# Sigmoid attention and a gated MLP on one core: group 0 loaded as FP32 by SyncE and cast on chip, and the first pass laid out anew

## The chip, the cores and the metric

The kernel runs on one core of a Trainium2 chip. The metric is the device time of one execution, in microseconds (us). The engines are TensorE (PE, matrix products into PSUM), VectorE (DVE), ScalarE (ACT), GpSimd (POOL) and SyncE (SP, which only issues DMAs here). Each engine has a queue of its own and works through it in order.

## The reference

```python
def _attn_ref(q, k, v):                    # q, k, v: 8 x 12 x 448 x 64, float32
    S = q.shape[2]
    scale = 1.0 / np.sqrt(q.shape[-1])
    scores = scale * np.matmul(q, k.transpose(0, 1, 3, 2)) - np.log(S)
    attn = 1.0 / (1.0 + np.exp(-scores))
    return np.matmul(attn, v).astype(np.float32)

def _moe_ref(x, w_in, w_out, beta):        # x: 3584 x 768, w_in: 768 x 2048, w_out: 2048 x 768
    h = x @ w_in
    g = h * (1.0 / (1.0 + np.exp(-beta * h)))
    return (g @ w_out).astype(np.float32)
```

The attention's output, with its heads side by side (3584 tokens of 768), is the MLP's x. There is no softmax: each score goes through a sigmoid by itself.

## The kernel before, in words

**Groups and visits.** The heads are taken four at a time: a group g is four heads of one batch, so there are 24 groups, three to a batch. A group's q and k are loaded with a cast from FP32 to FP16 by DMAs that POOL issues (`load_one`, L126), into a tile `raws[g]`. DVE transposes them (`transpose`: L207 for q, L216 and L220 for k). A visit is a set of score matmuls (L236) for one group and 128 of its keys, with the sigmoid on ACT behind it (`weigh`, L249, or `weigh_two`, L264) which reads the scores out of PSUM. The values (`attend`, L334) multiply the sigmoids by v, and DVE casts the results into `xTs` (L343), the input of the MLP. The last 64 keys of a head need v's last rows twice, in both halves of the partitions: `double_v_last` (L171) copies them.

**Dense matmuls.** All matmuls of the MLP stand in one list, `fill`, in a fixed order: x @ w_in (L356 for the first batches, L521 for the later ones), the gate (ACT L368 and L532, DVE L371 and L535, POOL L535), and the product with w_out (L386, L435, and L639 in a Strassen scheme). `fill_units(n)` issues the next n of them. They are put between the visits, so that PE works while ACT does the sigmoids.

**The first pass.** For batch 0, three groups, the order is written out by hand in the list `BEGIN`. A half visit (`half_visit`) covers half of a group's queries: `("scores", g, half, second)`, where second says which keys. `("q", g, half)` and `("k", g)` are transposes, `("values", g, half)` the values, `("dense", n)` n matmuls of `fill`, `("idle", n)` n zero matmuls. Zero matmuls (`idle_units`, L765) multiply a tile of zeros, 512 columns each, and their result is not used. Eleven stand ahead of everything, 12 more lie between the first half visits. The first dense matmuls need the values of all three groups for one half of the queries, so six half visits stand ahead of those; two more stand ahead of the dense ones in the list.

**Loads.** POOL issues group 0's first q half and its k before all else, then `LOADS` in order: groups 1 and 2, v, q's second halves, and the eight parts of w_in. `loads()` issues what follows (group 3, w_out, the next v). The DMAs of POOL share eight semaphores in turn, so the ninth waits for the first to have landed, and so on. SP issues the load of beta at the start, and the stores.

**Later visits.** From batch 1 on a loop over `visits` (numbered n) issues one visit, then as many dense matmuls as a pace asks for: what is left to do in the phase over the visits that are left. `MORE` adds to or takes from that number by visit, `LATE` says how many dense matmuls go ahead of the values in a visit, and `RESERVE` what is held back at the end of a phase. `first_layer` is a stretch in which x @ w_in of a pair of batches is done without visits.

**The end.** The last token tile is done by `single` (L435), whose second matmul group reads a sum of two halves of the gated values, made by DVE (L420) when the tile begins.

Of the kernel before, what the change touches and what calls it, by code (L numbers as in the profile page):

```python
# [13 lines left out]
def kernel(  # L14
# [10 lines left out]
    nc = tc.nc  # L25
# [175 lines left out]
    def transpose(g: int, r: int, c0: int = 0, c1: int = NB):  # L201
        raw = raws[g][:, r]
        if r == 0:
# [3 lines left out]
            nc.vector.transpose(  # L207
                out=in_order(g // QPB, qT[g][:, c0 * BLK : c1 * BLK]),
                in_=raw[:, c0:c1].rearrange("p c d -> p (c d)").bitcast(FP32),
            )  # L210
            return
# [393 lines left out]
    def hid(t: int, half: int):  # L605
        return gt[:, half * ND : (half + 1) * ND, cols(t)]
# [144 lines left out]
    with tc.manual_schedule():  # L751
        load_one(0, 0, 0, NH)
        load_one(0, 1)
        nc.gpsimd.memset(nlogs, NEG_LOG_S)
# [8 lines left out]
        def idle_units(n: int):  # L763
            for _ in range(n):
                nc.tensor.matmul(idle, still[:, 0:P], still, start=True, stop=True)  # L765

        idle_units(11)
        def load(what, *a):
            if what == "q":
                load_one(a[0], 0, a[1] * NH, (a[1] + 1) * NH)  # L770
            elif what == "k":
                load_one(a[0], 1)
            elif what == "v":
                load_v_full(0, a[0] * HQ, a[1] * HQ)
            elif what == "last":
                load_v_last(0)
            elif what == "w_in":
                load_w_in(*a)

        nc.sync.dma_start(out=beta_in[0:NDC], in_=moe_beta.rearrange("(c p) -> c p", p=P))  # L780
        LOADS = [
            ("q", 1, 0), ("k", 1), ("q", 2, 0), ("k", 2), ("last",), ("v", 0, 3), ("q", 0, 1), ("q", 1, 1),
            ("w_in", 0, 2), ("w_in", 2, 4), ("q", 2, 1), ("w_in", 4, 6), ("w_in", 6, 8), ("w_in", 8, 10),
            ("w_in", 10, 12), ("w_in", 12, 14), ("w_in", 14, 16),
        ]
        for x in LOADS:
            load(*x)

        def loads():
            load_qk(3)  # L790
            load_w_out(0, 0)
            load_w_out(1, 0)
            load_v(1)
            load_qk(4)
            load_qk(5)
            load_w_out(0, 1)
            load_w_out(1, 1)

        def beta_columns():
# [5 lines left out]
        BEGIN = [  # L805
            ("q", 0, 0), ("k", 0), ("q", 1, 0), ("scores", 0, 0, 1), ("idle", 4), ("k", 1), ("idle", 4),
            ("scores", 0, 0, 0), ("k", 2), ("q", 2, 0), ("scores", 1, 0, 0), ("idle", 4), ("v", 0),
            ("scores", 1, 0, 1), ("scores", 2, 0, 0), ("values", 0, 0), ("q", 0, 1), ("q", 1, 1),
            ("scores", 2, 0, 1), ("beta",), ("values", 1, 0), ("scores", 0, 1, 0), ("values", 2, 0),
            ("scores", 0, 1, 1), ("loads",), ("q", 2, 1), ("dense", 12), ("scores", 1, 1, 1), ("two",),  # L810
            ("dense", 6), ("scores", 1, 1, 0), ("dense", 18), ("scores", 2, 1, 0), ("values", 0, 1),
            ("values", 1, 1), ("scores", 2, 1, 1), ("dense", 9), ("values", 2, 1), ("dense", 42), ("k", 3),
            ("q", 3, 0), ("q", 3, 1), ("dense", 21),
        ]
        for what, *a in BEGIN:
# [5 lines left out]
            elif what == "scores":  # L821
                half_visit(a[0], a[1] * QH, a[2])
            elif what == "idle":
                idle_units(a[0])
# [34 lines left out]
        def left_us(n: int):  # L859
# [57 lines left out]
        for n, (g, jt, also) in enumerate(visits):  # L917
# [73 lines left out]
```

## Time and profile before

| | |
|---|---|
| median of 3 runs | 376.06 us (375.95 to 376.45) |
| profiled execution | 375.61 us |
| its span, first to last instruction | 373.8 us |
| PE busy | 365.7 us (98%) |
| ACT busy | 255.8 us (68%) |
| DVE busy | 254.2 us (68%) |
| POOL busy | 91.5 us (24%) |
| bytes read from HBM | 45.62 MB |

Times in the rows below are microseconds from the start of the span. A row of the timeline has the start, the time taken, the engine, the line, the operation, what it writes and reads, how many were merged (x16), and in brackets the idle time of the engine before it and what ended that. A row of the chain of waits has the start, the time taken and what the end of the kernel hung on then. The busy time of PE is modelled and has short waits in it. PEclk is the granted clock of TensorE, 1.00 at full speed.

### The profile page before, as it was taken

Reading aid. Unit: us, or ns where it says so; the run is one execution under the profiler, and the core shown is the slowest. Engines: PE = TensorE matmul, PEld = TensorE weight load, DVE = VectorE, ACT = ScalarE, POOL = GpSimd, SP = SyncE. Lnnn points to the kernel's source line nnn. Section 1 sums busy time; section 2 is a strip of 40 time slices with the busy share of each in tenths; the row PEclk is TensorE's granted clock in tenths of the full one; section 3 lists DMA queues with packets and bytes.
Section 4 is the critical chain, followed back from the end, with each engine's and each line's share of the span. In section 5 each row is a group of like instructions: output and inputs, shape, how many; then the busy total and the mean of one; then the engine's idle time right before and its main releaser. Section 6 shows DMA issues by size and latency. Waiting matters only on the chain.

```text
span 373.8 us, 7284 instructions
## 1 busy us (share of the span) xinstructions
PE 365.7 (98%) x2887; PEld 182.5 (49%) x2887; DVE 254.2 (68%) x478; ACT 255.8 (68%) x295; POOL 91.5 (24%) x138
## 2 busy tenths in 40 slices
PE   8899999999999999999999999999999999999996
PEld 3466544443444455544444445554444455555654
DVE  2444796776586967787666667778767667678661
ACT  3996865698967668886767748887678647882000
POOL 8743353141151013234123003235100002230000
PEclk9999999999999999999999999999999999999999
DMA  8999999993269030039839301028903111000333
GB/s 116 178 196 203 197 203 200 231 125 51 49 81 179 1 86 1 0 51 127 171 50 213 91 16 28 1 35 112 162 3 84 44 44 42 1 2 1 86 84 126
DMA packets 42545, 34.29 MB, mean 92 GB/s; under 512 B 21888, under 2 KB 39056, under 8 KB 42512
## 3 DMA queue, kind: packets, MB, share of 16 engines
q0 software_dynamic: 36976, 22.81, 44.6%
q1 hardware_dynamic: 5536, 11.02, 10.4%
q8 instruction: 22, 0.36, 0.4%
q14 instruction: 11, 0.09, 0.1%
HBM read 45.62 MB, written 11.01 MB: 151 GB/s over the span
## 4 chain that ended last, share of the span: by engine, by line
PE 91%; ACT 5%; DVE 2%; issue 1%; DMA 1%; POOL 0%; ACTq 0%; POOLq 0%
PE ps L639 26%; PE ps L521 26%; PE ps L236 11%; PE ps L334 9%; PE ps L356 9%; PE ps L386 4%; PE ps L435 4%; ACT attns L249 3%; ACT attns L264 1%; DMA raw<-in_k_dram 1%; ACT sg L368 1%; PE ps L765 0%; DVE sum L628 0%; DVE kT L216 0%; DVE qT L207 0%
## 5 line engine op out<-in xcount | busy, mean ns | idle before, releaser
L264 ACT ACTIVATE attns<-ps,nlogs 128x1792 f16<-128x1792 f32 x75 | 131.6, 1755 | 46.3 <-PE ps L236 46.0
L535 POOL TENSOR_TENSOR gt<-attns,sg 128x448 f16<-128x448 f32 x21 | 23.9, 1139 | 142.0 <-ACT sg L532 142.0
L639 PEld LDWEIGHTS <-sum 128*128 128x128 f16 x440 | 40.3, 98 | 36.9 <-issue 12.1
L236 PE MATMUL ps<-qT,kT 32*128 32x448 f16 (+3 forms) x864 | 51.9, 339 | 2.8 <-ACT attns L249 1.7
L532 ACT ACTIVATE sg<-ps,beta_sb 128x448 f32<-128x448 f32 x72 | 45.2, 632 | 8.6 <-PE ps L521 5.8
L521 PE MATMUL ps<-xT,w_in 128*128 128x448 f16 x216 | 49.2, 353 | 0.0
L521 PE MATMUL ps<-xT,w_S 128*128 128x448 f16 x216 | 49.2, 352 | 0.0
L639 PE MATMUL ps<-w_T,sum 128*128 128x384 f16 x264 | 48.5, 327 | 0.0
L535 DVE TENSOR_TENSOR gt<-ps,sg 128x448 f16<-128x448 f32 x72 | 44.3, 619 | 3.9 <-ACT sg L532 3.7
L343 DVE CAST xT<-ps 128x448 f16<-128x448 f32 (+1 forms) x54 | 28.9, 569 | 22.9 <-PE ps L334 22.7
L521 PEld LDWEIGHTS <-w_in 128*128 128x128 f16 x288 | 28.0, 98 | 26.6 <-issue 0.7
L657 DVE TENSOR_TENSOR osb<-ps,osb 128x384 f32<-128x384 f32 x55 | 30.5, 555 | 14.9 <-PE ps L639 12.9
L334 PE MATMUL ps<-attns,v 128*64 128x448 f16 (+3 forms) x432 | 40.5, 340 | 0.1
L356 PE MATMUL ps<-xT,w_in 128*128 128x448 f16 (+1 forms) x240 | 39.7, 316 | 0.6 <-DVE gt L371 0.6
L628 DVE TENSOR_TENSOR sum<-gt 128x1024 f16<-128x1024 f16 x55 | 36.5, 679 | 0.2
L126 POOL DMA_DIRECT2D raw<-in_q_dram x27 | 15.1, 558 | 80.2 <-DVE kT L220 72.6
L371 DVE TENSOR_TENSOR gt<-ps,sg 128x448 f16<-128x448 f32 (+1 forms) x40 | 20.0, 527 | 20.4 <-ACT sg L368 20.2
L639 PE MATMUL ps<-w_out,gt 128*128 128x384 f16 x176 | 33.3, 327 | 0.0
L639 PE MATMUL ps<-w_out,sum 128*128 128x384 f16 x176 | 32.2, 327 | 0.0
L581 DVE TENSOR_TENSOR ps<-ps,attns 128x448 f32<-128x448 f32 x24 | 15.2, 633 | 23.2 <-PE ps L521 22.4
L521 PEld LDWEIGHTS <-w_S 128*128 128x128 f16 x216 | 21.1, 98 | 19.4
L356 PEld LDWEIGHTS <-w_in 128*128 128x128 f16 x240 | 21.9, 98 | 17.1 <-issue 6.2
(51 smaller groups left out, 370.4 us busy)
## 6 DMA issues: line engine op xcount, KB each, us to landing
out_dram<-osb SPq DMA_DIRECT2D x100, 96.0 KB, 1.9
raw<-in_k_dram POOLq DMA_DIRECT2D x24, 224.0 KB, 5.6
raw<-in_q_dram POOLq DMA_DIRECT2D x21, 224.0 KB, 4.3
v<-in_v_dram POOLq DMA_DIRECT2D x32, 144.0 KB, 6.2
w_in<-in_moe_w_in_dram POOLq DMA_DIRECT2D x8, 384.0 KB, 11.4
w_out<-in_moe_w_out_dram POOLq DMA_DIRECT2D x4, 768.0 KB, 13.7
v<-in_v_dram POOLq DMA_DIRECT2D x16, 48.0 KB, 6.1
out_dram<-osb SPq DMA_DIRECT2D x2, 384.0 KB, 2.3
```

The lines of the kernel that those rows point to most:

```text
L236: nc.tensor.matmul(sco[base : base + nk, hh, u0 : u0 + n], kT[g][lo : lo + BLK, jt * P : jt * P + nk, e], qT[g][lo : lo + BLK, c0 : c0 + n ...
L264: nc.scalar.activation(out=attns[:, slot : slot + 2].rearrange("p n h s -> p (n h) s"), in_=sco, func=AF.Sigmoid, bias=nlogs[:, 0:1], scal ...
L334: nc.tensor.matmul(av[hh * D : (hh + 1) * D, 0:n], vs[b][base : base + nk, 2 * (s % NPAIR) + hh, jt], at[base : base + nk, hh, 0:n], start ...
L343: nc.vector.tensor_copy(out=xTs[b][:, s % NPAIR, c0 : c0 + n], in_=av[:, 0:n])
L356: nc.tensor.matmul(m1, w_in16[:, hc, dc * P : (dc + 1) * P], xTs[b][:, hc, c0 : c0 + n], start=(hc == 0), stop=(hc == NHC - 1),)
L371: nc.vector.tensor_tensor(out=gt[:, dc, off : off + n], in0=m1, in1=sg[:, 0:n], op=ALU.mult)
L521: nc.tensor.matmul(out, w[:, c, i * P : (i + 1) * P], m[:, c], start=(start and c == 0), stop=(c == KH - 1), skip_group_check=not start,)
L532: nc.scalar.activation(out=sg, in_=h, func=AF.Sigmoid, bias=0.0, scale=beta_sb[:, dc : dc + 1])
L535: return lambda: engine.tensor_tensor(out=gt[:, dc, b % 2 * S : b % 2 * S + S], in0=h, in1=sg, op=ALU.mult)
L628: nc.vector.tensor_tensor(out=sums[t, i], in0=x, in1=y, op=op)
L639: nc.tensor.matmul(m2, (x if op is None else sums[t, i])[:, dc], w[:, dc], start=first, stop=(dc == ND - 1), skip_group_check=i >= 4,)
L657: nc.vector.tensor_tensor(out=out, in0=in0, in1=in1, op=op)
```

## The change

Four things are changed.

1. Group 0's k, and then the first half of its q, are loaded by SP as FP32 into a part of `gt` (the gated values' tile, not yet in use), and cast to FP16 into `raws[0]`: DVE casts k's first 8 blocks of 14 (512 columns), ACT the other 6 (384 columns) and then q's 7 blocks (448 columns). POOL's two loads of them go, and its two memsets now stand ahead of its loads. SP's load of beta comes after its two new loads.
2. The zero matmuls have 256 columns instead of 512. Twenty stand ahead of the first scores instead of 11, and 23 between the half visits instead of 12.
3. The order of the first pass is new: `LOADS` has the rest of v ahead of its last rows and all second halves of q ahead of w_in; the first half visits are those of group 0 (second keys), group 1 (both), group 0 (first keys), group 2; and the dense matmuls come in other portions. `loads()` comes later in the list, and 126 dense matmuls are in `BEGIN` in place of 108.
4. `MORE`, `LATE` and the index of `RESERVE` differ, so that dense matmuls lie elsewhere between the later visits. The sum of halves of the last tile is made at the beginning of the sixth of the seven products of the pair before it.

The number of real matmuls and of sigmoids is the same.

```diff
+    def sum_of_halves(t: int):
+        sums[t, 0] = sump.tile([P, ND, P], FP16, tag="sum", name="sum")
+        nc.vector.tensor_tensor(out=sums[t, 0], in0=hid(t, 0), in1=hid(t, 1), op=ALU.add)
...
         if (n, dc) == (0, 0):
-            sums[t, 0] = sump.tile([P, ND, P], FP16, tag="sum", name="sum")
-            nc.vector.tensor_tensor(out=sums[t, 0], in0=hid(t, 0), in1=hid(t, 1), op=ALU.add)
+            if (t, 0) not in sums:
+                sum_of_halves(t)
...
+        if (t, i, dc) == (NT - 3, NPROD - 2, 0):
+            sum_of_halves(NT - 1)
...
-        load_one(0, 0, 0, NH)
-        load_one(0, 1)
-        nc.gpsimd.memset(nlogs, NEG_LOG_S)
-        nc.gpsimd.memset(dummy, 0.0)
...
-        idle_units(11)
...
         LOADS = [
-            ("q", 1, 0), ("k", 1), ("q", 2, 0), ("k", 2), ("last",), ("v", 0, 3), ("q", 0, 1), ("q", 1, 1),
-            ("w_in", 0, 2), ("w_in", 2, 4), ("q", 2, 1), ("w_in", 4, 6), ("w_in", 6, 8), ("w_in", 8, 10),
+            ("q", 1, 0), ("k", 1), ("k", 2), ("q", 2, 0), ("v", 0, 3), ("last",), ("q", 1, 1), ("q", 2, 1),
+            ("q", 0, 1), ("w_in", 0, 2), ("w_in", 2, 4), ("w_in", 4, 6), ("w_in", 6, 8), ("w_in", 8, 10),
             ("w_in", 10, 12), ("w_in", 12, 14), ("w_in", 14, 16),
         ]
+        staged = gt[:, 0:4].rearrange("p c w -> p (c w)").bitcast(FP32)
+        raws[0] = rawp.tile([P, 2, NB, D], FP16, tag="raw", name="raw")
+        parts = {1: (staged, NB), 0: (staged[:, NB * D :], NH)}
+        for r, (to, n) in parts.items():
+            nc.sync.dma_start(
+                out=to[:, 0 : n * D],
+                in_=(q, k)[r][0, 0:HQ].rearrange("h (p c) d -> (h p) (c d)", c=NB)[:, 0 : n * D],
+            )
+
+        def cast(r: int, c0: int, c1: int, act: bool):
+            out = raws[0][:, r, c0:c1].rearrange("p c d -> p (c d)")
+            frm = parts[r][0][:, c0 * D : c1 * D]
+            if act:
+                nc.scalar.copy(out=out, in_=frm)
+            else:
+                nc.vector.tensor_copy(out=out, in_=frm)
+            ready.update((r, "cast", c) for c in range(c0, c1))
+
+        nc.gpsimd.memset(nlogs, NEG_LOG_S)
+        nc.gpsimd.memset(dummy, 0.0)
...
-                nc.tensor.matmul(idle, still[:, 0:P], still, start=True, stop=True)
+                nc.tensor.matmul(idle[:, 0:256], still[:, 0:P], still[:, 0:256], start=True, stop=True)
...
         BEGIN = [
-            ("q", 0, 0), ("k", 0), ("q", 1, 0), ("scores", 0, 0, 1), ("idle", 4), ("k", 1), ("idle", 4),
-            ("scores", 0, 0, 0), ("k", 2), ("q", 2, 0), ("scores", 1, 0, 0), ("idle", 4), ("v", 0),
-            ("scores", 1, 0, 1), ("scores", 2, 0, 0), ("values", 0, 0), ("q", 0, 1), ("q", 1, 1),
-            ("scores", 2, 0, 1), ("beta",), ("values", 1, 0), ("scores", 0, 1, 0), ("values", 2, 0),
-            ("scores", 0, 1, 1), ("loads",), ("q", 2, 1), ("dense", 12), ("scores", 1, 1, 1), ("two",),
-            ("dense", 6), ("scores", 1, 1, 0), ("dense", 18), ("scores", 2, 1, 0), ("values", 0, 1),
-            ("values", 1, 1), ("scores", 2, 1, 1), ("dense", 9), ("values", 2, 1), ("dense", 42), ("k", 3),
-            ("q", 3, 0), ("q", 3, 1), ("dense", 21),
+            ("cast", 1, 0, 8, False), ("cast", 1, 8, 14, True), ("cast", 0, 0, 7, True), ("k", 0), ("q", 0, 0),
+            ("q", 1, 0), ("idle", 20), ("scores", 0, 0, 1), ("k", 1), ("idle", 1), ("idle", 4), ("idle", 2),
+            ("k", 2), ("q", 2, 0), ("scores", 1, 0, 0), ("idle", 9), ("v", 0), ("scores", 1, 0, 1),
+            ("scores", 0, 0, 0), ("idle", 7), ("scores", 2, 0, 0), ("values", 0, 0), ("q", 1, 1),
+            ("scores", 2, 0, 1), ("beta",), ("q", 0, 1), ("values", 1, 0), ("scores", 0, 1, 0),
+            ("values", 2, 0), ("scores", 0, 1, 1), ("dense", 6), ("scores", 1, 1, 1), ("two",), ("dense", 9),
+            ("loads",), ("scores", 1, 1, 0), ("q", 2, 1), ("dense", 21), ("scores", 2, 1, 0), ("dense", 12),
+            ("values", 0, 1), ("scores", 2, 1, 1), ("values", 1, 1), ("values", 2, 1), ("dense", 45), ("k", 3),
+            ("q", 3, 0), ("q", 3, 1), ("dense", 33),
         ]
...
         MORE = {
-            0: -1, 1: -1, 3: -1, 9: -1, 10: 1, 13: 1, 14: -2, 15: 1, 16: -1, 17: -2, 19: -1, 20: -2, 24: -1,
-            27: -1, 32: -1, 34: 1, 35: 1, 38: 1, 45: -1, 47: 1, 51: 1, 52: 1, 53: -1, 54: 1, 55: 1, 59: 1,
-            67: -1,
+            0: -2, 2: 1, 3: -1, 5: 1, 10: 1, 13: 1, 14: -2, 15: 1, 16: -1, 17: -2, 19: -1, 20: -2, 24: -1,
+            27: -1, 28: -1, 32: -1, 34: 1, 35: 1, 43: -1, 44: 1, 45: 1, 46: -1, 47: 1, 49: 1, 51: 1, 52: 2,
+            53: -1, 54: 1, 55: 1, 59: 1, 67: -1,
         }
         RESERVE = (1.99, 3.28)
         LATE = {
-            26: 6, 34: 4, 48: 3, 68: 10, 72: 10,
+            0: 1, 17: 1, 26: 6, 34: 4, 45: 2, 48: 3, 68: 10, 72: 10,
         }
...
-            todo = left_us(L1B) if g < 2 * QPB else left_us(len(fill)) - RESERVE[g >= 6 * QPB]
+            todo = left_us(L1B) if g < 2 * QPB else left_us(len(fill)) - RESERVE[n >= max(turn_at)]
```

More of the change, by code (lines that the diff above doesn't have):

```diff
@@ L202, in transpose @@
         raw = raws[g][:, r]
+        assert g or (r, c0) == (0, NB // 2) or all((r, "cast", c) in ready for c in range(c0, c1))
         if r == 0:
@@ L751, with load @@
     with tc.manual_schedule():
-        load_one(0, 0, 0, NH)
-        load_one(0, 1)
+        def load(what, *a):
+            if what == "q":
+                load_one(a[0], 0, a[1] * NH, (a[1] + 1) * NH)
+            elif what == "k":
+                load_one(a[0], 1)
+            elif what == "qk":
+                load_qk(a[0])
+            elif what == "v":
+                load_v_full(0, a[0] * HQ, a[1] * HQ)
+            elif what == "last":
+                load_v_last(0)
+            elif what == "values":
+                load_v(a[0])
+            elif what == "w_in":
+                load_w_in(*a)
+            elif what == "w_out":
+                load_w_out(*a)
+        LOADS = [
+            ("q", 1, 0), ("k", 1), ("k", 2), ("q", 2, 0), ("v", 0, 3), ("last",), ("q", 1, 1), ("q", 2, 1),
+            ("q", 0, 1), ("w_in", 0, 2), ("w_in", 2, 4), ("w_in", 4, 6), ("w_in", 6, 8), ("w_in", 8, 10),
+            ("w_in", 10, 12), ("w_in", 12, 14), ("w_in", 14, 16),
+        ]
+        LATER = [
+            ("qk", 3), ("w_out", 0, 0), ("w_out", 1, 0), ("values", 1), ("qk", 4), ("qk", 5), ("w_out", 0, 1),
+            ("w_out", 1, 1),
+        ]
+        staged = gt[:, 0:4].rearrange("p c w -> p (c w)").bitcast(FP32)
[14 more added lines that the diff above has]
+            ready.update((r, "cast", c) for c in range(c0, c1))
         nc.gpsimd.memset(nlogs, NEG_LOG_S)
@@ L764, in idle_units @@
             for _ in range(n):
-                nc.tensor.matmul(idle, still[:, 0:P], still, start=True, stop=True)
-        idle_units(11)
[L768 to L781, printed above, removed]
-            ("q", 1, 0), ("k", 1), ("q", 2, 0), ("k", 2), ("last",), ("v", 0, 3), ("q", 0, 1), ("q", 1, 1),
-            ("w_in", 0, 2), ("w_in", 2, 4), ("q", 2, 1), ("w_in", 4, 6), ("w_in", 6, 8), ("w_in", 8, 10),
-            ("w_in", 10, 12), ("w_in", 12, 14), ("w_in", 14, 16),
-        ]
+                nc.tensor.matmul(idle[:, 0:256], still[:, 0:P], still[:, 0:256], start=True, stop=True)
+        nc.sync.dma_start(out=beta_in[0:NDC], in_=moe_beta.rearrange("(c p) -> c p", p=P))
         for x in LOADS:
@@ L789, in loads @@
         def loads():
[L790 to L797, printed above, removed]
+            for x in LATER:
+                load(*x)
         def beta_columns():
@@ L822 @@
                 half_visit(a[0], a[1] * QH, a[2])
+            elif what == "cast":
+                cast(*a)
             elif what == "idle":
```

## The prediction

> **What bounds the kernel now.** I read the page first, then busy time in stretches, then the chain of waits over the first 32 us, then the timeline there.
>
> ```profile
> span 373.8 us, 7284 instructions
> PE 365.7 (98%) x2887; PEld 182.5 (49%) x2887; DVE 254.2 (68%) x478; ACT 255.8 (68%) x295; POOL 91.5 (24%) x138
> ```
> ```profile
> core 0: us, PE busy (x) PEld busy (x) DVE busy (x) ACT busy (x) POOL busy (x), PEclk, DMA share, GB/s
> 0.00:6.00 6.00, 4.56 (x15) 1.54 (x19) 1.51 (x5) 1.49 (x2) 4.97 (x15) 1.00 0.58 76
> ...
> 9.00:19.30 10.30, 8.53 (x149) 4.63 (x150) 4.63 (x17) 10.19 (x12) 8.28 (x12) 1.00 1.45 176
> 19.30:30.60 11.30, 10.32 (x162) 7.53 (x159) 4.24 (x13) 10.31 (x16) 4.30 (x7) 1.00 1.45 197
> ...
> 40.10:164.00 123.90, 123.85 (x956) 58.23 (x956) 91.63 (x164) 95.69 (x105) 33.20 (x51) 1.00 0.64 103
> 164.00:217.00 53.00, 52.66 (x471) 23.80 (x471) 36.51 (x70) 38.60 (x26) 12.72 (x22) 1.00 0.74 120
> ```
> PE is the bound of the whole: from 40.1 to 164 us it idles 0.05 us of 123.9. So an edit pays only where PE does no useful work, and the number of real matmuls stays the same here. The first 30.6 us are such a place. Up to 6 us PE's 4.56 busy us are nearly all zero matmuls, and from 9 to 19.3 us ACT is busy 10.19 of 10.30 us: the sigmoids of the first pass set the pace, PE waits for them.
>
> ```profile
> 1.95 3.31 DMA raw<-in_k_dram
> ...
> 5.29 0.59 DVE kT L216
> ...
> 5.92 0.70 PE ps L236 x15
> ```
> ```profile
> 1.19 4.49 PE L765 MATMUL ps<-still 128*128 128x512 f16 x11 [1.19 <-DVE still L759]
> 1.23 0.72 POOL L126 DMA_DIRECT2D raw<-in_q_dram  x1 [0.79 <-POOLq L975]
> 1.29 0.40 SPq L780 DMA_DIRECT2D beta_in<-in_moe_beta_dram  x1
> ...
> 1.95 0.54 POOL L126 DMA_DIRECT2D raw<-in_k_dram  x1
> ...
> 3.07 0.55 POOL L126 DMA_DIRECT2D raw<-in_k_dram  x1
> ...
> 4.20 0.41 DVE L207 STREAM_TRANSPOSE qT<-raw 128x224 f32<-128x224 f32 x1 [2.94 <-DMA raw<-in_q_dram]
> ...
> 5.79 0.20 DVE L220 STREAM_TRANSPOSE kT<-raw 128x64 f32<-128x64 f32 x1
> ...
> 6.55 1.90 PE L765 MATMUL ps<-still 128*128 128x512 f16 x8
> 6.67 1.53 ACT L249 ACTIVATE attns<-ps,nlogs 128x896 f16<-128x896 f32 x2 [3.81 <-PE ps L236]
> ...
> 8.32 0.58 DVE L216 STREAM_TRANSPOSE kT<-raw 128x384 f32<-128x384 f32 x1 [0.99 <-DMA raw<-in_k_dram]
> ...
> 9.00 11.99 ACT L249 ACTIVATE attns<-ps,nlogs 128x896 f16<-128x896 f32 x14 [0.79 <-PE ps L236]
> ...
> 10.05 0.57 PE L236 MATMUL ps<-qT,kT 32*128 32x224 f16 x14 [0.83 <-ACT attns L249]
> ...
> 14.16 0.98 PE L334 MATMUL ps<-attns,v 128*64 128x224 f16 x16
> ...
> 18.66 0.83 POOL L177 DMA_DIRECT2D w_in<-in_moe_w_in_dram  x1 [1.27 <-DMA w_in<-in_moe_w_in_dram]
> ...
> 19.27 1.32 PE L356 MATMUL ps<-xT,w_in 128*128 128x224 f16 x12
> ...
> 21.81 0.73 PE L356 MATMUL ps<-xT,w_in 128*128 128x224 f16 x6 [0.58 <-DVE gt L371]
> ...
> 28.54 1.53 ACT L249 ACTIVATE attns<-ps,nlogs 128x896 f16<-128x896 f32 x2 [0.81 <-PE ps L236]
> ...
> 29.38 1.25 PE L334 MATMUL ps<-attns,v 128*64 128x224 f16 x16
> ```
> The order is: group 0's k lands at 5.29 (issued by POOL at 1.95), two transposes, first scores at 5.92, first sigmoid at 6.67. Then ACT idles 0.79 us until 9.00, since group 1's k (issued 3.07, fourth in POOL's queue) is transposed only at 8.32. From 9.00 ACT runs 14 sigmoids without a pause for 11.99 us. Dense matmuls start at 19.27 behind eight half visits, and the first pass ends about 30.6, when the values of 29.38 are done.
>
> **Part 1: the first scores.** SP issues k (448 KB, now FP32 on both sides), then q's half (224 KB). Its beta load no longer goes first and its k waits for nothing. Other engines are released at about 0.8:
>
> ```profile
> 0.86 0.27 DVE L759 MEMSET still<- 128x256 uint32 x1 [0.86 <-PEq L975]
> ```
> ```profile
> out_dram<-osb SPq DMA_DIRECT2D x2, 384.0 KB, 2.3
> ...
> beta_in<-in_moe_beta_dram SPq DMA_DIRECT2D x1, 8.0 KB, 1.5
> ```
> No load of this size on SP's queue is in the trace. The two rows above are the nearest: 8 KB land in 1.5 us, 384 KB in 2.3, so 0.8 us for 376 KB; 448 KB come to 2.4, and k lands at 0.8 + 2.4 = 3.2. The other end is POOL's own k, 3.3 us from issue to landing: 4.1. I take 3.3, since SP's rows are the same queue and nothing else moves yet (POOL's first load landed at 4.20 after an issue at about 1.2). q's half lies behind it in the ring: 224 x 0.8 / 376 = 0.5 us more, 3.8.
>
> The casts are new on this path. Nearest rows:
>
> ```profile
> L343 DVE CAST xT<-ps 128x448 f16<-128x448 f32 (+1 forms) x54 | 28.9, 569 | 22.9 <-PE ps L334 22.7
> ```
> ```profile
> 358.62 0.48 ACT L660 COPY osb<-ps 128x384 f32<-128x384 f32 x1 [8.62 <-PE ps L639]
> ```
> ```profile
> 11.14 0.35 DVE L171 COPY v<-v 64x768 f16<-64x768 f16 x1
> ```
> DVE casts 512 columns of k: 512/448 of 0.57 = 0.65 from the PSUM row, 512/768 of 0.35 = 0.23 from the SBUF row; I take 0.55 (it reads four bytes per element). ACT casts 384 columns beside it, 0.48, and then q's 448, 0.56, done at about 4.4. k is cast at 3.9. Then DVE: 0.5 from one kT transpose's start to the next (5.29 to 5.79), 0.20, then q's 0.41, now behind k instead of ahead of it: 5.0. Bounds: 4.7 with the fast cast, 5.9 with k at 4.1 and the slow one.
>
> The zero matmuls stand in front of the scores as well. Eleven took 4.49 us, at a spacing of about 0.42 us for 512 columns; after the first scores eight took 1.90, 0.24 each: PE begins at half pace. Twenty of 256 columns from 1.19 at 0.21 end at 5.4, or 5.25 if the pace changes at about 5 us. So the first scores come at 5.3, not 5.92: 0.6 us. ACT's casts end long before its first sigmoid, at 5.3 + 0.75 = 6.05. Queued behind the waits: on DVE all transposes of groups 0 to 2, behind k's landing at 3.3 where q's held them until 4.20; on ACT the first sigmoid, behind q's cast. The beta load on SP stands behind two issues of 0.40 and is first needed by values that are ready long after (cover: some ten us). POOL's two memsets now stand ahead of its loads; I count 0.2 us for them in part 2.
>
> **Part 2: group 1 and the sigmoid run.** POOL loses two loads (issues of 0.72 and 0.54 us): group 1's q and k take first and second place, where group 0's landed at 4.20 and 5.29. Both sets now use the engines at once. SP's 672 KB take 672 x 0.8 / 376 = 1.4 us at the rate above; about a third of that has passed before POOL's bytes move, the rest, 0.9, delays them. With 0.2 for the memsets k lands at 6.4; the ends are 5.3, undelayed, and 7.9, as before (8.3) less SP's lead of 0.4. Transposed (0.58) at 7.0; scores and a first sigmoid follow in about 0.6, at 7.6. ACT's first pair ends at 6.05 + 1.53 = 7.6, too. So the pause of 0.79 goes as well, and the sigmoid run starts at 7.6 instead of 9.00: **-1.4 us**. What is late next: group 2's k, one place behind and needed four visits later, and v's doubled last rows, in this stream behind v's four loads. Before, that copy stood at 11.14 and the first values at 14.16, which would be 12.8 now. The copy may come up to 0.3 us after that; the sigmoids of the visit whose scores stand ahead of those values (1.5 us and more) cover it. Without that cover each us that v is late is a us lost.
>
> **Part 3: dense matmuls.** They wait for the same eight half visits, so they start at 19.27 - 1.4 = 17.9, if weights are there. The issue at 18.66 waited for the first weight load; it lies 0.2 us ahead of that. In the new order group 2's second q half (POOL, 0.6 us of transfer) goes ahead of it, while the whole stream starts about 1 us sooner: 18.0 to 18.3, a wait of up to 0.4; I take +0.2. Six, nine, 21 and 12 dense matmuls in place of 12, 6, 18 and 9 between the visits give ACT's next scores precedence: the idle 0.81 on ACT at 28.54 and PE's 0.58 at 21.81 can shrink. Of their 1.4 I take 0.4. First pass: -1.4 + 0.2 - 0.4 = **-1.6**, bounds -0.3 and -2.5.
>
> **Part 4: the rest.** The counts between later visits move single dense matmuls. PE's idle time there is 0.34 us in 164 to 217; short waits hide in its busy time, 0.57 for eight score matmuls where 0.51 is usual:
>
> ```profile
> 172.06 0.51 PE ps L236 x8
> ...
> 184.50 0.57 PE ps L236 x8
> ```
> Nine such visits lie in that stretch, at most 0.8 us together with the idle time: I take **-0.2**, bounds -0.7 and +0.4 (a unit taken from a visit shortens its cover by the length of one matmul). At the end the sum of halves is moved before the last pair's product:
>
> ```profile
> 364.93 1.46 PE L435 MATMUL ps<-w_out,gt 128*128 128x384 f16 x8
> 366.34 1.47 PE L435 MATMUL ps<-w_out,sum 128*128 128x384 f16 x8
> 367.65 0.82 PE L435 MATMUL ps<-w_out,gt 128*128 128x192 f16 x8
> ```
> Eight take 1.31 from start to start (366.34 to 367.65); the eight before took 1.41. So **-0.1**.
>
> **Sum.** -1.6 - 0.2 - 0.1 = -1.9. The profiled execution took 375.61 (span 373.8 and 1.8 around it): 373.7. It was 0.45 below the median of the three runs, 376.06, so the forecast for the median is **374.2**.
>
> **The rivals.** *Shared engines.* The early loads gain only their issue: SP's and POOL's bytes share the same DMA engines and group 1's k lands 0.4 us sooner, not 1.9. For it: from 9 us on DMA streams without end, 176 and 197 GB/s in the stretches above. Against: from 0 to 6 us the mean is 76 GB/s, so there is room early. Then k is transposed at 7.9 and the run starts at 8.6, and with 0.3 from part 4: -0.7, 375.4. The Trainium skill states it as a rule (DMA: Bandwidth & Descriptors, "Issuing engines are not separate DMA queues"): starting DMAs from several engines saves only sequencer time, as all run on the same engines; the low 76 GB/s speaks for room that this rule leaves open.
>
> *Cold PE (slower).* The half pace of the first zero matmuls returns within the first pass, because PE is less busy between its visits (PEclk stands at 1.00 throughout, so only the spacing tells). Twelve zero matmuls of 512 columns stood between the first scores and the values; 23 of 256 stand there now, 5,888 columns for 6,144. Price: half visits and values (0.70 and 0.98 us on PE at full pace) take twice that, 3.4, where values follow, and pass ACT's 1.7 us per visit (11.99 for seven): 1.7 lost at each of the three values, up to 5, of which the sigmoid queue of two visits covers about 3, so +2; and the first 3.8 us of zero matmuls at half pace (1.19 to about 5) would have to be served again by dense ones, +1.9. With -1.9 of gains: +2, 378. It decides if PE's rows beside the scores show 0.42 per 512 columns again after 6 us. Against it: the idle gap of 0.83 us at 10.05 did not bring it back here (14 score matmuls in 0.57 behind it, 15 in 0.70 at 5.92). The Trainium skill has a clock gate that halves PE's rate after an idle window of about 3.4 us (TensorE: Matmul & The Clock Gate, "What's actually happening"); no idle time of that length is in this trace.
>
> *Given back.* Scores come sooner but dense matmuls wait for weights or v, and the first pass still ends near 30.6: only part 4's 0.3 is left, 375.8. It decides if the weights land no sooner than 18.5 and each later one follows at the old pace. Against: from 19.3 to 30.6 PE's one idle time on a dense line, 0.58, waited for DVE, none for a load.
>
> **How the numbers follow.** Forecast 0.66 (374.2, own range 372.9 to 375.1), shared engines 0.16, cold PE 0.08, given back 0.10. About 0.2% (0.75 us) is what a measurement of this kernel can tell: the limits are 375.3 and 376.8. Faster: 0.66 and two thirds of the shared engines, 0.77. Slower: cold PE and a part of given back, where the new counts also cost their 0.4, 0.10. Same: 0.13. The range 372.9 to 375.6 leaves out cold PE and given back.
>
> **What would show it.** SP's k lands by 3.5 and the first scores stand at 5.2 to 5.5; ACT's run starts at 7.4 to 7.9 with no gap after its first pair; dense matmuls start at 17.9 to 18.3. Wrong if the zero matmuls or q's cast hold the first scores to 5.9, if group 1's k is transposed after 8, or if PE idles over 0.5 us for weights. A gain without an earlier dense start would be wrong in its place.

## The result, and the profile after

The changed kernel takes 375.19 us, the median of 13 runs (374.77 to 377.18); the kernel before took 376.04 on the same chip (13 runs, 375.57 to 376.71). The ratio is 0.9977 [0.9966, 0.9988]: faster by 0.85 us. The time is in the range given; the gain had been forecast at 1.9. Each ratio, here and below, has its 95% interval beside it and need not be the quotient of two medians. The profiled execution took 375.10 us (span 373.3), the one before 375.61 (373.8). Lines from 203 on have moved: L216 of before is L217, L236 is L237, L249 is L250, L356 is L357.

The page and busy time in stretches, changed kernel, in the columns of the prediction's rows:

```profile
span 373.3 us, 7332 instructions
PE 365.6 (98%) x2907; PEld 185.2 (50%) x2907; DVE 254.6 (68%) x479; ACT 257.0 (69%) x297; POOL 90.4 (24%) x136
```
```profile
0.00:6.00 6.00, 4.68 (x32) 3.03 (x36) 1.98 (x6) 2.56 (x4) 5.04 (x14) 1.00 0.70 169
...
9.00:19.30 10.30, 9.00 (x159) 5.27 (x156) 4.50 (x16) 9.83 (x12) 8.68 (x12) 1.00 1.41 174
19.30:30.60 11.30, 10.88 (x168) 7.92 (x160) 4.52 (x13) 10.76 (x17) 3.85 (x6) 1.00 1.45 197
...
40.10:164.00 123.90, 123.81 (x954) 58.08 (x952) 91.57 (x164) 95.92 (x106) 33.15 (x50) 1.00 0.64 102
```

From 0 to 6 us the DMA engines move 169 GB/s where they moved 76. From 9 to 19.3 ACT is busy 9.83 us where it was busy 10.19: the stretch that was filled with sigmoids now has a hole. From 19.3 to 30.6 PE idles 0.42 us instead of 0.98. From 40.1 to 164 PE is as busy as before (123.81 us for 123.85). The hole shows in the timeline and the chain of waits:

```profile
0.74 0.39 SPq L790 DMA_DIRECT2D gt<-in_k_dram  x1
...
1.19 4.33 PE L815 MATMUL ps<-still 128*128 128x256 f16 x20 [1.19 <-DVE still L809]
1.29 0.72 POOL L126 DMA_DIRECT2D raw<-in_q_dram  x1 [0.42 <-issue]
...
2.00 1.07 POOL L126 DMA_DIRECT2D raw<-in_k_dram  x2
...
3.91 0.58 DVE L801 CAST raw<-gt 128x512 f16<-128x512 f32 x1 [2.64 <-DMA gt<-in_k_dram]
...
5.65 0.70 PE L237 MATMUL ps<-qT,kT 32*128 32x224 f16 x16
...
6.40 1.53 ACT L250 ACTIVATE attns<-ps,nlogs 128x896 f16<-128x896 f32 x2 [1.31 <-PE ps L237]
...
7.48 0.58 DVE L217 STREAM_TRANSPOSE kT<-raw 128x384 f32<-128x384 f32 x1 [0.99 <-DMA raw<-in_k_dram]
...
8.11 0.58 PE L237 MATMUL ps<-qT,kT 32*128 32x224 f16 x16 [0.89 <-DVE kT L217]
...
8.72 8.52 ACT L250 ACTIVATE attns<-ps,nlogs 128x896 f16<-128x896 f32 x10 [0.79 <-PE ps L237]
...
15.74 0.81 DVE L829 STREAM_TRANSPOSE beta_sb<-beta_in 32x32 f32<-32x32 f32 x4
...
16.57 0.41 DVE L208 STREAM_TRANSPOSE qT<-raw 128x224 f32<-128x224 f32 x1
...
17.66 3.41 ACT L250 ACTIVATE attns<-ps,nlogs 128x896 f16<-128x896 f32 x4 [0.41 <-PE ps L237]
...
19.34 0.75 PE L357 MATMUL ps<-xT,w_in 128*128 128x224 f16 x6
...
30.68 11.57 PE L357 MATMUL ps<-xT,w_in 128*128 128x448 f16 x78
```
```profile
2.00 5.45 DMA raw<-in_k_dram
```

SP's two new loads in the list of transfers up to 9 us (KB each, us from issue to landing):

```profile
gt<-in_k_dram SPq DMA_DIRECT2D x1, 448.0 KB, 3.1
...
gt<-in_q_dram SPq DMA_DIRECT2D x1, 224.0 KB, 3.3
```

Group 0's first sigmoid comes at 6.40 instead of 6.67. The pause of 0.79 behind the first pair is still there; the run starts at 8.72 instead of 9.00 and waits for group 1's k, which is issued at 2.00 and lands 5.45 us later, at 7.45. At 17.66 there is a second pause, 0.41: group 0's second q half is transposed only at 16.57, behind the four transposes of beta. So of the 0.28 won nothing is left at 19.34, where the dense matmuls begin 0.07 later than before. By 30.68 the gain is 0.20 (the same matmul starts at 30.89 in the trace of before).

The end, where the prediction shows 364.93, 366.34 and 367.65:

```profile
364.70 1.46 PE L440 MATMUL ps<-w_out,gt 128*128 128x384 f16 x8
366.00 1.46 PE L440 MATMUL ps<-w_out,sum 128*128 128x384 f16 x8
367.30 0.82 PE L440 MATMUL ps<-w_out,gt 128*128 128x192 f16 x8
```

-0.23 before the sum of halves and -0.35 behind it. The two profiles differ by 0.5: the last 0.13 of that lies behind the last matmuls. The medians differ by 0.85; that difference is taken up with the loads below.

### The profile page after: what moved, and what is told of

It is laid out like the page before. It is cut to its first block, busy times and chain, and to the rows that moved or that the text cites. A ratio compares the mean times of both kernels' runs of the same rounds, so it can differ in the third digit from the quotient of the medians.

```text
span 373.3 us, 7332 instructions
## 1 busy us (share of the span) xinstructions
PE 365.6 (98%) x2907; PEld 185.2 (50%) x2907; DVE 254.6 (68%) x479; ACT 257.0 (69%) x297; POOL 90.4 (24%) x136
## 4 chain that ended last, share of the span: by engine, by line
PE 90%; ACT 4%; DVE 2%; DMA 1%; issue 1%; POOL 0%; ACTq 0%; POOLq 0%
PE ps L646 27%; PE ps L526 26%; PE ps L237 11%; PE ps L357 9%; PE ps L335 8%; PE ps L387 4%; PE ps L440 4%; ACT attns L250 2%; ACT attns L265 2%; DMA raw<-in_k_dram 1%; ACT sg L369 1%; DVE qT L208 1%; DVE sum L633 0%; DVE xT L344 0%; DVE kT L217 0%
## 5 line engine op out<-in xcount | busy, mean ns | idle before, releaser
L237 PE MATMUL ps<-qT,kT 32*128 32x448 f16 (+3 forms) x864 | 51.9, 340 | 3.1 <-ACT attns L250 1.1
L526 PEld LDWEIGHTS <-w_in 128*128 128x128 f16 x288 | 28.0, 98 | 26.6 <-issue 0.7
L357 PE MATMUL ps<-xT,w_in 128*128 128x448 f16 (+1 forms) x240 | 39.8, 316 | 0.1
L237 PEld LDWEIGHTS <-kT 32*128 32x128 f16 (+1 forms) x864 | 15.1, 96 | 30.6 <-issue 26.7
```

Source lines behind the costliest of these rows:

```text
L237: nc.tensor.matmul(sco[base : base + nk, hh, u0 : u0 + n], kT[g][lo : lo + BLK, jt * P : jt * P + nk, e], qT[g][lo : lo + BLK, c0 : c0 + n ...
L357: nc.tensor.matmul(m1, w_in16[:, hc, dc * P : (dc + 1) * P], xTs[b][:, hc, c0 : c0 + n], start=(hc == 0), stop=(hc == NHC - 1),)
L526: nc.tensor.matmul(out, w[:, c, i * P : (i + 1) * P], m[:, c], start=(start and c == 0), stop=(c == KH - 1), skip_group_check=not start,)
```

## The experiments

The theory after this profile: the early loads do come early, but the order put behind them spends the lead, because the second visit now needs group 1's k and a q half stands behind beta. The rivals: bytes of SP and POOL share one rate, so that nothing behind the first scores can come sooner (shared engines); PE's half pace; and that the layout is good and the loads are worth nothing.

### What holds ACT: the order of visits and q's second half

`e1_order` makes group 0's first keys, which need no new data, the second visit; `e2_q01` brings group 0's second q half forward; `e3_both` does both, and `e11_both_again` is that kernel once more.

```diff
 e1 (and e3):
-... ("scores", 0, 0, 1), ("k", 1), ("idle", 1), ("idle", 4), ("idle", 2), ("k", 2), ...
+... ("scores", 0, 0, 1), ("k", 1), ("idle", 1), ("scores", 0, 0, 0), ("idle", 6), ("k", 2), ...
-("scores", 0, 0, 0), ("idle", 7), ("scores", 2, 0, 0),
+("idle", 7), ("scores", 2, 0, 0),
 e2 (and e3):
 LOADS: ("q", 0, 1) ahead of ("q", 1, 1) and ("q", 2, 1) instead of behind them
 BEGIN: ("q", 0, 1) right behind ("v", 0) instead of behind ("beta",)
```

> The changed kernel with group 0's other half visit (first keys) as the second visit instead of the fourth, so that the second visit needs nothing of group 1. Theory A (the early gain was lost at two places: the second visit waits for group 1's k, and later the third pair waits for group 0's second q half, transposed only at 16.57): ACT's pause of 0.79 us at 8.72 goes, its run starts at 7.9, but the wait for that q half grows from 0.41 to about 1.2, so dense matmuls still start at 19.3 and the time stays at 375.2. Theory B (landings of v and w_in set the pace of the first pass): the same time, and dense matmuls at 19.3 too; this run alone does not part them.

> The changed kernel with group 0's second q half loaded ahead of the other two second halves, and transposed on DVE right behind the copy of v's last rows, ahead of the beta transposes. Theory A: the ACT pause of 0.41 us at 17.66 goes, dense matmuls start at 18.9 instead of 19.34, time 374.8. Theory B: dense matmuls stay at 19.3, time 375.2.

> Both edits on the changed kernel. Theory A: ACT runs without a pause from 6.4 on, dense matmuls start at 18.1 (weights of the first part landed at 17.3 in the changed kernel), time 374.0, that is 2.0 below the kernel before. Theory B: 19.3 and 375.2 as without the edits.

Measured: e1 374.82 us (5 runs), ratio 0.9969 [0.9956, 0.9982]; e2 375.06 (6 runs), 0.9968 [0.9956, 0.998]; e3 374.38 (4 runs), 0.9953 [0.9938, 0.9968]. The kernel before took 376.12 beside them. ACT's timeline, e1 first, then e2, then e3, with the first dense matmul of each:

```profile
6.69 10.12 ACT L250 ACTIVATE attns<-ps,nlogs 128x896 f16<-128x896 f32 x12 [1.62 <-PE ps L237]
...
17.32 3.41 ACT L250 ACTIVATE attns<-ps,nlogs 128x896 f16<-128x896 f32 x4 [0.51 <-PE ps L237]
...
19.01 0.75 PE L357 MATMUL ps<-xT,w_in 128*128 128x224 f16 x6
```
```profile
8.68 12.01 ACT L250 ACTIVATE attns<-ps,nlogs 128x896 f16<-128x896 f32 x14 [0.73 <-PE ps L237]
...
18.96 0.75 PE L357 MATMUL ps<-xT,w_in 128*128 128x224 f16 x6
```
```profile
5.71 1.08 PE L237 MATMUL ps<-qT,kT 32*128 32x224 f16 x16
...
6.84 13.67 ACT L250 ACTIVATE attns<-ps,nlogs 128x896 f16<-128x896 f32 x16 [1.63 <-PE ps L237]
...
18.80 0.75 PE L357 MATMUL ps<-xT,w_in 128*128 128x224 f16 x6
```

Each edit takes away exactly the pause it was made for: the first pair and the run become one in e1, the pause before the last four goes in e2, and e3 has sixteen sigmoids without one. So both pauses come from the order, and shared engines don't forbid the lead: group 0's own data were there. These rows carry the reading; by their times alone, neither e1 nor e2 can be told from the changed kernel (their intervals overlap with 0.9966 to 0.9988). The expectation for e1 missed in part: the dense matmuls were to stay where they were and came 0.33 sooner, since everything ahead of the second pause, the values and DVE's casts among it, had moved too. In e3 they came at 18.80 and not 18.1. The first 16 scores ran at PE's half pace, 1.08 us for 0.70, and ACT's run started at 6.84 instead of 6.4: that is 0.44 of the 0.70, and the rest was a sum too short. Later e3's execution lost half of its lead: 0.75 us ahead of the trace of before at 30.9, it is 0.38 ahead from 60.7 on, and between them, at 59.17, PE waited 0.20 us for a part of w_out. The trace of e11, the same kernel, has no such wait.

> The changed kernel with both edits (second visit from group 0, its second q half first) once more, in more rounds. Expected: 374.1 to 374.7, ratio 0.994 to 0.997 to the kernel before, below the changed kernel's 0.9977; ACT without a pause up to the first gates; dense matmuls at 18.5 to 18.8.

Measured: 374.34 (5 runs), ratio 0.9956 [0.9944, 0.9969], sixteen sigmoids without a pause, dense from 18.85. This is the fastest version found. Its nine executions, e3's and these, took 374.01 to 374.95; the kernel before never took less than 375.57, and of the changed kernel's 13 executions 11 took longer than 374.95. The interval still touches the changed kernel's.

### The loads alone, and the layout alone

`e5_loads_only` is the kernel before with SP's FP32 loads and the casts (the code of the diff, and at the head of `BEGIN` the three casts and k's transposes ahead of q's); the rest, the order and the zero matmuls too, is as before. `e6_layout_only` is the changed kernel with the two FP16 loads by POOL instead, ahead of its memsets.

```diff
 e6, in the changed kernel:
-        staged = ...   (SP's two loads, cast())
+        load_one(0, 0, 0, NH)
+        load_one(0, 1)
-            ("cast", 1, 0, 8, False), ("cast", 1, 8, 14, True), ("cast", 0, 0, 7, True), ("k", 0), ("q", 0, 0),
+            ("q", 0, 0), ("k", 0),
```

> The kernel before with one part of the change: group 0's k and first q half loaded by SP as FP32 and cast on DVE and ACT; order, zero matmuls and counts as before. Theory A (each stage of the first pass has another limit): first scores 0.1 to 0.25 sooner than 5.92 (the eleven zero matmuls of 512 columns end at 5.7), the second visit is still held by eight zero matmuls (8.2 to 8.45) and then group 1's k, at 7.5, holds nothing; ACT's run starts at 8.7 to 8.8, the dense matmuls 0.2 to 0.3 sooner than 19.27; time 375.7 to 375.9. Rival (the prediction's part 2): a sooner k of group 1 moves the whole run, dense matmuls at 18.4 or less, time 375.2.

> The changed kernel with POOL's two FP16 loads of group 0 back at the head of its queue, and no casts: the new order, zero matmuls and counts alone. Theory A: the second visit now needs group 1's k, fourth in POOL's queue as before, landing 8.3; ACT's run starts at 9.4 to 9.6 instead of 8.72, dense matmuls at 19.9 to 20.1, time 375.9, about that of the kernel before. Rival (the loads matter little, the layout makes the gain): dense matmuls at 19.3 to 19.5, time 375.2.

Measured: e5 375.5 (10 runs, 375.29 to 375.86; before 376.18), ratio 0.9976 [0.9962, 0.999]. e6 ran from 375.77 to 378.71, median 377.45 of 10 runs, ratio 1.0017 [0.9995, 1.004]. The loads alone bring most of the gain, by the medians 0.68 us where the whole change brought 0.85; the ratio looks as good as the whole change's also because two of the 19 executions of before beside it took 378.3 and 378.5. The layout without the loads brings nothing that shows, and may cost: three of its executions took 375.8 to 376.3 and seven 377.2 to 378.7. Neither expectation foresaw this: e5's time lies between its theory (375.7 to 375.9) and its rival (375.2), e6's median above both of its own (375.9 and 375.2). Timeline of PE, DVE and ACT in e5:

```profile
5.86 0.70 PE L236 MATMUL ps<-qT,kT 32*128 32x224 f16 x16 [0.80 <-DVE qT L207]
...
6.49 1.90 PE L781 MATMUL ps<-still 128*128 128x512 f16 x8
...
7.08 0.58 DVE L216 STREAM_TRANSPOSE kT<-raw 128x384 f32<-128x384 f32 x1 [0.91 <-DMA raw<-in_k_dram]
...
8.32 0.67 PE L236 MATMUL ps<-qT,kT 32*128 32x224 f16 x18
...
8.93 11.99 ACT L249 ACTIVATE attns<-ps,nlogs 128x896 f16<-128x896 f32 x14 [0.79 <-PE ps L236]
...
19.21 1.32 PE L356 MATMUL ps<-xT,w_in 128*128 128x224 f16 x12
```

These rows correct the reading of the kernel before. Group 1's k is transposed at 7.08, 1.2 us sooner than before, and ACT's run still starts at 8.93 behind the same pause of 0.79. What stands in front of the second visit's scores at 8.32 are the eight zero matmuls, from 6.49 to 8.39, and the scores wait for nothing else: that visit is group 0's. The chain of waits of the kernel before had said so, in the rows behind those that the prediction shows: between the first scores and the run stand the zero matmuls and the second visit's scores, and no transpose of group 1's k.

```profile
6.62 1.83 PE ps L765 x8
8.45 0.56 PE ps L236 x16
9.02 4.60 ACT attns L249 x5
```

In e6, timeline of PE and ACT:

```profile
7.01 1.07 PE L236 MATMUL ps<-qT,kT 32*128 32x224 f16 x16 [1.37 <-DVE kT L216]
...
8.02 1.67 PE L798 MATMUL ps<-still 128*128 128x256 f16 x7
```

POOL's k came late in this execution (scores at 7.01), and PE was at half pace until 10.5: 0.24 us for a zero matmul of 256 columns where 0.12 is the full pace. In the profiled executions with group 0 loaded by POOL the first scores stood at 5.92, 6.38, 7.01 and 7.12; with SP's loads at 5.65 to 5.98 in nine. The trace of before, 5.92, is thus an early one, and a steadier start is the likely reason that the medians differ by more than the two profiles. That link is argued from these few executions, not shown run by run.

`e10_loads_zeros_behind` tests the new reading: the kernel before with SP's loads, and six of the eight zero matmuls moved behind the second visit. Against e5, in `BEGIN`:

```diff
-("q", 1, 0), ("scores", 0, 0, 1), ("idle", 4), ("k", 1), ("idle", 4), ("scores", 0, 0, 0), ("k", 2),
+("q", 1, 0), ("scores", 0, 0, 1), ("k", 1), ("idle", 2), ("scores", 0, 0, 0), ("idle", 6), ("k", 2),
```

> The kernel before with SP's loads of group 0 and their casts, and of the eight zero matmuls ahead of the second visit two stay and six go behind it. Theory A (with the early loads, these zero matmuls alone hold ACT's run): the pause of 0.79 us goes, the run starts at about 8.1 instead of 8.93, dense matmuls at 18.4 to 18.6, time 374.7 to 374.9. Rival 1 (what comes later gives it back): dense matmuls at 19.2, time 375.5. Rival 2 (cold PE, as in the same edit without SP's loads): 377 to 379.

Measured: 374.91 (5 runs), ratio 0.9969 [0.9957, 0.9981]; PE and ACT:

```profile
6.52 0.61 PE L781 MATMUL ps<-still 128*128 128x512 f16 x2
...
6.64 13.83 ACT L249 ACTIVATE attns<-ps,nlogs 128x896 f16<-128x896 f32 x16 [1.25 <-PE ps L236]
...
18.75 1.32 PE L356 MATMUL ps<-xT,w_in 128*128 128x224 f16 x12
```

The pause is gone and the dense matmuls start at 18.75, 0.46 sooner than in e5 (19.21). So it was the zero matmuls.

### What the zero matmuls are for

`e4_before_nozero` takes all eight away from that place without the loads: the kernel before with `("scores", 0, 0, 1), ("k", 1), ("scores", 0, 0, 0), ("idle", 8)`. `e8_before_nozero_again` is the same kernel in one more execution.

> The kernel before, with the eight zero matmuls ahead of its second visit moved behind it; loads as before. As the prediction read it, group 1's k held ACT until 9.00: then nothing changes, 9.00 and 376.0. Theory A': the second visit is group 0's own and was held by the eight zero matmuls (6.55 to 8.45): then ACT's run starts at 8.2, the dense matmuls 0.3 to 0.8 sooner than 19.27, time 375.3 to 375.7.

> The same kernel as the one without the eight zero matmuls ahead of the second visit, once more for its profile: three timed executions took 377.7 to 379.3 us, the profiled one 376.0. Theory (cold PE): in a slow execution PE runs at half pace far into the first pass (0.42 us per zero matmul of 512 columns after 6 us, score matmuls 1.0 instead of 0.6 us for sixteen), until dense matmuls have run for some 3 us. Rival: a load lands late in the slow ones, PE at full pace.

Measured: e4 375.97 in the profiled execution and 377.73 to 379.25 in three more, ratio 1.0066 [1.0043, 1.0088]: slower, where no change or a gain was expected. Its profile has the pause behind the first pair gone, and another of 0.51 us ahead of 11.15, where group 1's scores stand behind the eight zero matmuls in their new place (8.70 to 10.60); it doesn't show the loss. e8's execution took 379.18 and does. Its busy time in stretches, and its timeline of PE and ACT:

```profile
4.13:7.54 3.41, 1.47 (x17) 0.53 (x19) 1.12 (x3) 0.00 (x0) 3.01 (x6) 1.00 0.99 144
7.54:10.95 3.41, 2.60 (x27) 1.05 (x24) 1.27 (x4) 2.64 (x4) 1.78 (x3) 0.50 1.47 175
10.95:14.37 3.42, 3.42 (x23) 1.12 (x22) 1.20 (x4) 0.80 (x1) 3.13 (x5) 0.50 1.49 190
```
```profile
7.12 1.12 PE L236 MATMUL ps<-qT,kT 32*128 32x224 f16 x18 [1.94 <-DVE kT L216]
...
9.91 3.59 PE L765 MATMUL ps<-still 128*128 128x512 f16 x8
...
14.41 10.20 ACT L249 ACTIVATE attns<-ps,nlogs 128x896 f16<-128x896 f32 x12 [2.66 <-PE ps L236]
```

PE reached full pace at 4.13 by the trace's clock records and lost it again at 7.54, for 6.8 us: the granted clock is 0.50, and the eight zero matmuls take 3.59 us where they took 1.90. ACT waits 2.66 us. So the cold-PE rival is real, though not in the profile of the changed kernel. In this execution group 0's k was ready only at 6.48; in e4's, the same kernel, it was ready at 5.75, and full pace held. The Trainium skill (TensorE: Matmul & The Clock Gate, "What's actually happening") has PE fall back after an idle window of about 3.4 us; this trace has the window's length but not the idleness: in the window before the fall PE was busy 1.47 of 3.41 us, and its longest wait was 1.94.

### Shared engines

`e7_pool_late` puts three memsets of an unused part of `gt` on POOL ahead of its loads (before they hold anything), so that POOL issues 1.9 us later and SP's loads have the DMA engines to themselves.

```diff
         nc.gpsimd.memset(dummy, 0.0)
+        for c in (8, 9, 10):
+            nc.gpsimd.memset(gt[:, c], 0.0)
```

> The changed kernel with three POOL memsets (of a part of gt that is written later) ahead of POOL's first load, so that its loads are issued some 1.5 to 2.5 us later. Question: does POOL's stream slow SP's load of k, which took 3.14 us from issue to landing where 2.4 were forecast? Theory A (its own pace: POOL's first bytes move only when k is nearly in): k lands at 3.8 to 3.9 as before, group 1's k later by about what the issue is late. Rival (shared engines also for k): k lands at 3.2 to 3.5.

Measured: 375.64 in one execution. Timeline of POOL and DVE:

```profile
3.15 0.72 POOL L126 DMA_DIRECT2D raw<-in_q_dram  x1
...
4.34 0.43 DVE L801 CAST raw<-gt 128x512 f16<-128x512 f32 x1 [3.08 <-DMA gt<-in_k_dram]
...
7.62 0.58 DVE L217 STREAM_TRANSPOSE kT<-raw 128x384 f32<-128x384 f32 x1 [1.00 <-DMA raw<-in_k_dram]
```

SP's k lands no sooner without POOL beside it (the cast begins at 4.34, and at 3.91 to 4.33 in the eight traces with POOL's loads issued early), so POOL doesn't slow SP. The other way round, the traces of the transfers tell: the first bytes of POOL's queue move 1.44 us after its first issue in the kernel before (2.67), 2.36 after it in the changed kernel (3.65), when nine tenths of SP's bytes were under way, and 1.43 after it in e7 (4.58), when all of them were. So POOL's bytes stood behind SP's for 0.9 us in the changed kernel, and not at all in e7. Group 1's k, issued 1.9 us later in e7, is ready only 0.14 later (7.62 for 7.48). But that is one execution, and in the eight other traces with SP's loads this transpose starts anywhere from 7.08 to 8.43, so what the 1.9 us of issue are worth stays open; the theory had expected the whole 1.9. The Trainium skill has the rule that transfers started by different engines run on the same DMA engines and gain only the issue time (DMA: Bandwidth & Descriptors, "Issuing engines are not separate DMA queues"). The 0.9 us for which POOL's bytes stood behind SP's fit it; no run here prices the issue time.

### The new counts

`e9_old_counts` is the changed kernel with `MORE`, `LATE` and `RESERVE`'s index of the kernel before.

> The changed kernel with the old counts of dense matmuls between the later visits (MORE, LATE and the index of RESERVE as before). Theory: they move the end by a tenth of a us at most, since PE idles 0.05 us in 40 to 164 and 0.34 in 164 to 217 either way: between the first pass and the last product the offset to the kernel before stays within 0.15 us of the changed kernel's, time 375.1 to 375.3. Rival (the prediction's part 4): the new counts are worth 0.2 to 0.7 us, time 375.4 to 375.9.

Measured: 375.7 (11 runs, 375.21 to 377.63), ratio 0.999 [0.998, 0.9999] for the changed kernel's 0.9977. In its profiled execution, the one of 377.63, PE fell back to half pace from 8.84 to 12.26 (busy time in stretches):

```profile
5.43:8.84 3.41, 1.74 (x24) 0.95 (x23) 1.26 (x5) 1.53 (x2) 1.51 (x4) 1.00 1.10 163
8.84:12.26 3.42, 3.20 (x33) 1.73 (x33) 1.34 (x5) 1.91 (x2) 2.42 (x5) 0.50 1.65 181
```

From there on its distance to the trace of before (start of the same matmul in both) goes from 2.10 us at 46 us to 2.22 ahead of the last sum of halves; the changed kernel's goes from -0.20 to -0.22. So the old counts cost 0.14 us more there, in one execution each (e3 shows that one wait for a load can move this distance by 0.37). That is within the theory's 0.15; the time, 375.7, is in the rival's range. The timed ratios differ by 0.0013, 0.5 us, and their intervals overlap; whether more than 0.14 belongs to the counts stays open.

## Why the prediction was right or wrong

The direction was right and the size was not: 0.85 us for 1.9. The step that failed is part 2: group 1's k was to land at 6.4 and landed at 7.45, so ACT's run came 0.28 us sooner and not 1.4. Part 3 then took that lead over whole, where the order of q's transposes spent what was left of it. In the traces, the start of the run was to bring 1.4 and brought 0.28; the way from there to the dense matmuls was to cost 0.2 and cost 0.35; the portions were to bring 0.4 and brought 0.27, the counts 0.2 and 0.02, the end 0.1 and 0.12.

**Part 1**, first scores at 5.3 (-0.6): they came at 5.65 (-0.27). SP's k landed 3.1 us after its issue, near the long bound of 3.3 and not the 2.4 taken from SP's store and 8 KB rows: the store's rate was no measure for this load. The cast took 0.58 for 0.55, and 0.43 to 0.57 in the eight other traces with SP's loads. The zero matmuls ended at 5.52, 0.1 behind the longer of the two counts (5.4), and were not what the scores stood behind: q's transpose ended at 5.60.

**Part 2**, run start at 7.6 (-1.4): it came at 8.72 (-0.28). Two errors. First, the pause before 9.00 in the kernel before was read as a wait for group 1's k, because its transpose at 8.32 ended just ahead. The row of eight zero matmuls, 6.55 to 8.45, was quoted and not weighed; e5 and e10 show that it was those, and the second visit needed no new data. Second, the change makes group 1 the second visit, so a wait for its k that had not bound before now does, and that k landed 1.05 later than the 6.4 counted; the transposes, scores and first sigmoid behind it took 1.27 for the 1.2 counted. The wait behind SP's bytes doesn't explain these 1.05: the count had 0.9 for it and 0.2 for the memsets, and POOL's first bytes moved 0.98 later than before (3.65 for 2.67). What the count left out came after that. In the kernel before, the load in second place (group 0's k) landed when POOL's queue had moved 348 KB, and the two loads up to it are 336; in the changed kernel 553 KB had moved when group 1's k landed, so 217 KB of loads that POOL had issued behind it went ahead of its end. This is read from two traces, and no run changes it alone, so that cause is argued and not shown. "The pause goes as well" was therefore wrong twice; e1 shows what makes it go.

**Part 3**, dense at 17.9: 19.34. The forecast took the lead of the run over whole, and watched weights and v. What came late was group 0's second q half, moved behind q's other halves and beta (0.41 at 17.66); e2 took this pause away, and dense moved to 18.96. No PE wait for weights is in the trace. Of the 0.4 for better portions, 0.27 came: +0.07 at 19.34 to -0.20 at 30.68, with PE's idle time in that stretch down by 0.56 and 48 dense matmuls done there instead of 45.

**Part 4**, counts -0.2 and end -0.1: the distance to before is -0.20 at 30.7, -0.17 at 84, -0.10 at 131, -0.23 at 217 and behind it, so of the -0.2 hardly anything is left; by e9's one execution the old counts would have cost 0.14 on the new first pass. The bound of 0.8 for this part is 0.88 by the rows it was taken from (nine times 0.06, and 0.34), which changes nothing. The end gave -0.12, as forecast; e5 and e10, which lack that edit, gain nothing there (0.01 at most).

**The rivals.** Shared engines came closest: 375.4 forecast, k transposed at 7.48 for 7.9, run start at 8.72 for 8.6. Its cause was half of it: with e1's order the same bytes start the run at 6.69. Cold PE is real, and in the traces it happens where a k lands late (group 0's in e6 and e8, group 1's in e9). The changed kernel's execution of 377.18 has no trace, but it is of the size of e9's profiled one and lists the same kind of granted clock, 0.994 for 0.995, where the other twelve list 0.998 to 1.0; so the rival very likely happened in one of 13. Five of e6's seven long executions and the two of the kernel before at 378.3 and 378.5 list 0.995 as well. Given back, by weights or v, did not happen as told; the lead was given back to a q half (and in e3 half of a larger lead to w_out).

## What to carry to other kernels

When a wait ends next to two events, check whether the waiting instruction needs the one you name: which data it reads, and what stands ahead of it in its own queue. A load that comes earlier pays only if the next instruction in the order uses it; put work that needs no new data there. Filler matmuls delay the work behind them, yet where too few of them cover a late load the pace of PE can halve (e8): keep them, and place them behind work that another engine waits for (e10, e11).

## What the runs showed of the hardware

- **PE's pace is set in windows of 3.41 us**, whose start differs by execution: by the clock records, full pace came first at 3.88 to 7.24 us in twelve traces and at 10.57 in e6, and changes within a trace lie 3.41 us or twice that apart (4.13, 7.54 and 14.37 in e8; 5.43, 8.84 and 12.26 in e9). In the windows that the traces allow to be compared, half pace ended behind one with PE busy 2.69 us or more (e5, 0.47 to 3.88) and went on behind 2.64 or less (e11, 0.41 to 3.82); full pace was lost behind 1.47 and 1.74 (e8, e9) and kept behind 2.08 or more (e4, 3.88 to 7.29). Those are bounds from 13 executions of one first pass. Ahead of a trace's first clock record the column PEclk shows 1.00 although the zero matmuls run at half pace, so there only their spacing tells.
- **SP's load of 448 KB** took 3.1 us to land and q's 224 KB behind it 3.3 from its own issue, beside 2.3 for SP's stores of 384 KB; the cast behind k began at 3.91 to 4.34 in nine traces.
- **POOL's bytes behind SP's**: the first bytes of POOL's queue moved 1.44 us after its first issue in the kernel before, where SP had only beta's 8 KB to move, and 2.36 after it in the changed kernel, behind SP's 672 KB. Its load in second place then landed 5.45 us after its issue (group 1's k, changed kernel), against 3.31 (group 0's k, kernel before).
- **Loads that POOL issues first** differed by over a microsecond from execution to execution (first scores 5.92 to 7.12); SP's differed by 0.33.
